# Sparse attention and a feed-forward layer on one core: a second reading for the range of the weight words, gamma folded into the first weights, one chunk more by seven products

## The chip, the cores and the metric

The kernel runs on one core of a Trainium2 chip. Its time is the device time of one execution in microseconds. Of the core's engines, TensorE (PE in the profile) multiplies matrices into PSUM, VectorE (DVE), ScalarE (ACT) and GpSimd (POOL) work on rows of 128 partitions, and SyncE (SP) issues most DMAs. Each engine runs its own row of instructions in a fixed order and waits for the others by semaphores.

## The reference

```python
scores = scale * np.matmul(q, k.transpose(0, 1, 3, 2))
keep = is_global | is_local              # k < n_global, or 0 <= q - k < n_local
bias = -slopes[:, None, None] * dist[None, :, :]
a = softmax(np.where(keep, scores + bias, -1e9))
x = np.matmul(a, v)                      # B 4, H 8, S 768, D 64: x is 4 x 768 x 512
xn = (x - mu) / np.sqrt(var + 1e-06) * g_ln
return x + np.maximum(xn @ w_ch1, 0.0) @ w_ch2   # 512 -> 2048 -> 512
```

The two counts come as 64-bit integers (8 and 96 here). The two weight matrices come as float64 words, which the chip has no arithmetic for. All else is float32.

## The kernel before

The 3072 tokens make 24 tiles of 128. A tile needs the keys of its own and of the previous tile, and the first 16 columns of its batch's first tile as global keys. The first tile of each batch is a "short" one: its scores need one block of keys. The four short tiles come first and are worked in float32 (`quick`): `tk` and `tq` are transposes of keys and queries on TensorE, `s` the scores, `T` their masked and exponentiated values (a custom step on VectorE adds the mask and finds the row's extreme), `tp` the transposed probabilities, copied to `pT`, `pv` probabilities by values, `x` the divided sum, `xs` the centred rows, `tx` their transposes. The other 20 tiles are split into pairs of float16 (upper and lower half: `kn`, `qn`, `vn`, `pn`, `xn`) and transposed by DMA. A pair of tiles is a chunk; its normalised, transposed rows are `xT`.

The weights are brought as 16 pieces of 1 MB (`wb0` to `wb15`, eight for each matrix). From a piece, ScalarE takes the low word (`wr`), VectorE the sign (`ws`), ScalarE the absolute high word with a running sum (`wz`, into `big`, from which the range of the words is judged at the end), VectorE shifts the two together (`ww`) into a float32 word, and the halves are written: the upper by any of three engines (`wu`: `w1h`, `w2h`), the lower by VectorE or GpSimd (`wl`: `w1l`, `w2l`). The pieces of the second matrix lie until their turn in `w2h`, `w2l` or `st`, which is why early rows of the first matrix's words carry the name `w2h`.

Each of the 12 chunks has eight first products F (24 products of 256 columns each, in `f`), whose rectified halves are `h`, and eight second products. For chunks below EVEN these are G (12 products of 512 columns); from EVEN on they are N, the "seven products": sums of h rows (`R`, made by `mixes`, then split into `uh` and `ul`) against sums of weight blocks (`va`, `t`; made once, by `sums_of_weights`), 21 products of 256 columns a step, in `m`. `combine` drains their sums into `x`, which SP stores.

The order of all of this is written out by a planner (`class Plan`): each piece of work is a task with an engine (or a choice of engines), a cost, a rank, the tasks that it follows and the buffers that it takes; the planner lists tasks greedily and each engine's row is then fixed. Where its TensorE would idle before UNTIL = 90, it puts filler products, `blank`. A helper, `Lane`, records every operation, so nearly all rows of the profile have its line, L204 (L238 in the kernel after). The last task but one is a flag: `judge` collects whether the counts, the words' range and the variances lie within what this path handles, `pf` adds that over the partitions with a product, and a branch to a general kernel follows (not taken here).

## Time and profile before

| | us |
|---|---|
| three runs, median (lowest to highest) | 608.58 (607.15 to 609.28) |
| profiled execution's span | 605.5 |
| TensorE busy | 591.0 (98%) |
| VectorE busy | 514.9 (85%) |
| ScalarE busy | 408.6 (67%) |
| GpSimd busy | 160.8 (27%) |

The span runs from the first to the last instruction of one profiled execution; the run's time holds some 3 us more. A busy TensorE counts filler products too, and the busy shares are means over stages of different kinds, so a stage is read by itself: the stages here are the start with the short tiles and first weights (to 73 us), the chunks with plain second products and attention (to about 230), those with seven products and attention (to about 510), and the rest without attention. The clock that TensorE was granted is 1.00 in all of them but the last, where it is 0.98.

### The profile page before, as it was taken

The page shows a single profiled execution, that of the slowest core. Times are in us where ns is not written, and L with a number is a line of the kernel's source. Part 1 is how long each engine was busy: PE and PEld are TensorE (multiplying, and loading weights), DVE is VectorE, ACT ScalarE, POOL GpSimd, SP SyncE. Part 2 cuts the span into 40 slices and gives each one's busy share as a digit, 9 for nine tenths or more (in the row PEclk, how much of TensorE's full clock was granted, in tenths as well). Part 3 has the DMA queues.
Part 4 walks back from the last instruction along what each step waited for, and adds up shares of the span by engine and source line. Part 5 has one row for each costly group of instructions (what it writes and reads, how often), then busy time and mean ns, then how long its engine had stood idle before and what let it go on. Part 6 is the DMA issues. An engine that isn't in the chain of part 4 may idle for free.

```text
span 605.5 us, 15320 instructions
## 1 busy us (share of the span) xinstructions
PE 591.0 (98%) x5929; PEld 489.7 (81%) x5929; DVE 514.9 (85%) x1244; ACT 408.6 (67%) x1004; POOL 160.8 (27%) x128
## 2 busy tenths in 40 slices
PE   8989999999999999999999999999999999999996
PEld 4767896556965985789999999999999999988885
DVE  5999999999999989899789999898898788484654
ACT  5988897965677865787765766889856756333330
POOL 2310121306463228242042122152232031040100
PEclk9999999999999999999999999999999999999999
DMA  8993999976879985977748676868865423110001
GB/s 217 321 312 102 238 221 193 244 183 132 221 165 183 183 191 130 202 158 108 156 125 141 139 157 123 162 137 160 154 141 123 105 55 88 36 40 16 35 2 37
DMA packets 247307, 88.33 MB, mean 146 GB/s; under 512 B 237376, under 2 KB 237376, under 8 KB 247232
## 3 DMA queue, kind: packets, MB, share of 16 engines
q1 hardware_dynamic: 246944, 87.32, 65.6%
q8 instruction: 47, 0.77, 0.6%
q14 instruction: 28, 0.23, 0.1%
q10 hardware_dynamic: 288, 0.00, 0.0%
HBM read 38.01 MB, written 6.29 MB: 73 GB/s over the span
## 4 chain that ended last, share of the span: by engine, by line
PE 62%; DVE 5%; DMA 1%; issue 1%; ACT 0%; DVEq 0%
PE f L204 31%; PE m L204 24%; PE s L204 4%; PE pv L204 3%; DMA out_dram<-x 1%; DVE vn L204 1%; DVE T L204 1%; DVE pn L204 1%; DVE x L204 1%; DMA xT<-xn 0%; DVE w2l L204 0%; DVE R L204 0%; DVE xs L204 0%; DVE qn L204 0%; DVE xn L204 0%
## 5 line engine op out<-in xcount | busy, mean ns | idle before, releaser
L204 PE MATMUL f<-xT,w1h 128*128 128x256 f16 x1536 | 256.3, 273 | 4.7 <-DVE xT L204 2.1
L204 PE MATMUL f<-xT,w1l 128*128 128x256 f16 x768 | 209.3, 273 | 0.0
L204 PEld LDWEIGHTS <-w1h 128*128 128x128 f16 x1536 | 147.5, 98 | 21.9 <-DVE xT L204 2.2
L204 DVE SCALAR_TENSOR_TENSOR R<-f,R 128x128 f32<-128x128 f32 x256 | 68.3, 288 | 35.0 <-ACT R L204 29.6
L204 PEld LDWEIGHTS <-uh 128*128 128x128 f16 x896 | 85.9, 98 | 9.4
L204 PEld LDWEIGHTS <-w1l 128*128 128x128 f16 x768 | 75.1, 98 | 9.2 <-issue 0.5
L204 ACT ACTIVATE T<-T,mn 128x256 f32<-128x256 f32 x160 | 80.1, 501 | 3.2
L204 PE MATMUL f<-w2h,h 128*128 128x512 f16 x256 | 80.4, 379 | 0.4 <-DVE h L204 0.4
L204 ACT ACTIVATE uh<-R 128x896 f16<-128x896 f32 x57 | 54.0, 948 | 38.2 <-DVE R L204 37.9
L204 DVE CUSTOM_DVE_ANT_0 T<-s,mask 128x256 f32<-128x256 f32 (+1 forms) x192 | 68.1, 396 | 10.8 <-PE s L204 10.7
L204 ACT ACTIVATE R<-f 128x512 f32<-128x512 f32 x59 | 35.1, 594 | 61.8 <-PE f L204 60.3
L204 PE MATMUL m<-w2h,uh 128*128 128x256 f16 x256 | 69.8, 273 | 0.0
L204 PE MATMUL m<-w2l,uh 128*128 128x256 f16 x256 | 69.8, 273 | 0.0
L204 PE MATMUL m<-w2h,ul 128*128 128x256 f16 x256 | 69.8, 273 | 0.0
L204 PE MATMUL m<-t,uh 128*128 128x256 f16 x384 | 69.5, 273 | 0.0
L204 PEld LDWEIGHTS <-h 128*128 128x128 f16 x384 | 36.3, 98 | 40.0 <-issue 0.6
L204 POOL TENSOR_TENSOR ul<-R,uh 128x896 f16<-128x896 f32 x17 | 32.4, 1907 | 121.4 <-ACT uh L204 121.4
L204 DVE TENSOR_TENSOR ul<-R,uh 128x896 f16<-128x896 f32 x47 | 54.1, 1151 | 12.1 <-ACT uh L204 11.8
L204 POOL TENSOR_TENSOR pn<-T,pn 128x512 f16<-128x512 f32 x27 | 33.8, 1250 | 114.0 <-ACT pn L204 90.1
L204 PE MATMUL s<-kT,qT 128*128 128x128 f16 (+1 forms) x704 | 55.7, 225 | 2.0 <-ACT T L204 0.9
L204 PE MATMUL m<-t,ul 128*128 128x256 f16 x192 | 52.3, 273 | 0.0
L204 ACT ACTIVATE pn<-T 128x512 f16<-128x512 f32 x78 | 48.7, 624 | 2.2 <-DMA xT<-xn 1.1
(155 smaller groups left out, 1018.3 us busy)
## 6 DMA issues: line engine op xcount, KB each, us to landing
st<-in_moe_w_ch_dram SPq DMA_DIRECT2D x10, 1024.0 KB, 6.8
kf<-in_k_dram SPq DMA_DIRECT2D x28, 256.0 KB, 3.9
vf<-in_v_dram SPq DMA_DIRECT2D x28, 256.0 KB, 3.4
qf<-in_q_dram SPq DMA_DIRECT2D x24, 256.0 KB, 3.2
out_dram<-x SPq DMA_DIRECT2D x24, 256.0 KB, 2.4
qT<-qT SPq DMA_DIRECT2D x40, 128.0 KB, 2.7
w2h<-in_moe_w_ch_dram SPq DMA_DIRECT2D x3, 1024.0 KB, 7.3
w2l<-in_moe_w_ch_dram SPq DMA_DIRECT2D x3, 1024.0 KB, 8.3
```

Source lines behind the costliest of these rows:

```text
L204: ins = getattr(self.engine, name)(*args, **kw)
```

## The change

- Chunk 3 has seven products instead of plain ones (EVEN 3), so the weight sums are due a chunk earlier.
- The reading of the high words on ScalarE (`wz`) goes, and `big` with it. Instead, all weights are read from memory once more behind the last tile's scores: 64 DMAs of 256 KB (`again`) and 64 steps on VectorE that collect exponent bits in `seen`, judged by `judge_words` before the flag's product.
- Gamma is multiplied into the first weights (`gw`, from a load `gs` of four elements a partition), so `gb`, a load of 256 KB, goes; the centring step now takes mean and root at once, so the diagonal matrix and its step go and `tx` is a plain transpose.
- The first two pieces of w1 hold 256 columns of all 512 rows instead of 512 columns of 256 rows ("tall"); the first F needs one of them. The halves of w1 are written by blocks of rows, each with its gamma. `wl` no longer has GpSimd as a choice.
- The counts are read to one partition and spread to all by a product (`all<-cnt,row`).
- The copy of global values (`gv`) is a DMA instead of a VectorE step. The mixes are three steps instead of four. In the last chunk product 3 has a bank with product 7, and the last stored piece is half a row block.
- The planner has other costs and ranks, tables that shift ranks by kind, and a changed LEAD (how many steps ahead the late tiles' scores may come). The sign step is on VectorE in both.

```diff
+WORD = -WS * 2.0 ** -128
...
-EVEN = 4
-EARLY = 150.0
-LEAD = 11
+EVEN = 3
+EARLY = -167.15
+LEAD = 4
...
+KINDS = {
+    "kh": 14.0, "vh": 10.0, "ph": 20.0, "wr2": 9.0, "pt": 33.0, "wl1": -13.0, "wb1": 3.0, "wu1": 13.0, "R": -10.0, "Z": -23.0, "vl": 23.0,
...
+    def asked(n):
+        src = (n_global, n_local)[n]
+        if "asked" not in made:
+            made["asked"] = const.tile([1, 2, 2], I32, name="nn")
+        act.dma_start(out=made["asked"][:, n, :], in_=src.bitcast(I32).partition_broadcast(1))
+
+    def count_one():
+        made["one"] = counted(const, vec, made["asked"])
+
+    def count_all():
+        made["all"] = ps_v.tile([P, 2], F32, tag="pv", name="all")
+        pe.matmul(made["all"], lhsT=made["row"], rhs=made["one"], start=True, stop=True)
 
     def count():
-        cnt = made["cnt"] = counted(const, vec, made["asked"])
+        cnt = made["cnt"] = const.tile([P, 2], F32, name="cnts")
+        vec.tensor_copy(out=cnt, in_=made["all"])
...
+    task("gs", "SP", 0.6, lambda: load.dma_start(out=gs, in_=g_ln.rearrange("(c p) -> p c", p=P)), rank=-5, dma=0.3)
+    task("gw", "DVE", 0.11, lambda: vec.tensor_scalar(out=gw, in0=gs, scalar1=WORD, scalar2=None, op0=ALU.mult), ["gs"], rank=-5)
...
+        tall = n < 2
+        if tall:
+            sl, cs = slice(n * 256, (n + 1) * 256), slice(0, NK)
+            src, dh, dl = w1[:, sl], w1h[:, :, sl], w1l[:, :, sl]
...
-        def sizes():
-            hi = staged[n][1]
-            act.activation(out=hi.bitcast(F32), in_=hi.bitcast(F32), func=AF.Abs, scale=2.0 ** -111, accum_out=big[:, n:n + 1])
-
         def whole():
             lo, hi, _, _ = staged[n]
-            vec.scalar_tensor_tensor(out=hi, in0=hi, scalar=3, in1=lo, op0=ALU.logical_shift_left, op1=ALU.bitwise_or)
+            vec.scalar_tensor_tensor(out=hi, in0=hi, scalar=3, in1=lo, op0=ALU.logical_shift_left, op1=ALU.bitwise_xor)
 
         def upper(engine):
-            if engine == "DVE":
-                vec.tensor_copy(out=dh, in_=staged[n][3])
+            word = staged[n][3]
+            if n < NF // 2:
+                if engine == "POOL":
+                    pool.tensor_tensor(out=dh, in0=word, in1=gw[:, cs].unsqueeze(2).to_broadcast(list(word.shape)), op=ALU.mult)
+                    return
+                for a in range(cs.stop - cs.start):
+                    g_ = gw[:, cs.start + a:cs.start + a + 1]
+                    if engine == "DVE":
+                        vec.tensor_scalar(out=dh[:, a], in0=word[:, a], scalar1=g_, scalar2=None, op0=ALU.mult)
+                    else:
+                        act.activation(out=dh[:, a], in_=word[:, a], func=AF.Copy, scale=g_)
+            elif engine == "DVE":
+                vec.tensor_scalar(out=dh, in0=word, scalar1=WORD, scalar2=None, op0=ALU.mult)
             elif engine == "POOL":
-                pool.tensor_tensor(out=dh, in0=staged[n][3], in1=fill.unsqueeze(2).to_broadcast([P, 2, 512]), op=ALU.subtract)
+                pool.tensor_scalar(out=dh, in0=word, scalar1=WORD, scalar2=None, op0=ALU.mult)
             else:
-                act.activation(out=dh, in_=staged[n][3], func=AF.Copy)
-
-        def lower(engine):
-            (pool if engine == "POOL" else vec).tensor_tensor(out=dl, in0=staged[n][3], in1=dh, op=ALU.subtract)
+                act.activation(out=dh, in_=word, func=AF.Copy, scale=WORD)
+
+        def lower():
+            word = staged[n][3]
+            if n < NF // 2:
+                for a in range(cs.stop - cs.start):
+                    k0 = cs.start + a
+                    vec.scalar_tensor_tensor(out=dl[:, a], in0=word[:, a], scalar=gw[:, k0:k0 + 1], in1=dh[:, a], op0=ALU.mult, op1=ALU.subtract)
+            else:
+                vec.scalar_tensor_tensor(out=dl, in0=word, scalar=WORD, in1=dh, op0=ALU.mult, op1=ALU.subtract)
...
-        task(f"ws{n}", "DVE", 0.7, signs, [f"wr{n}"], rank=rank, port=True)
-        task(f"wz{n}", "ACT", 1.2, sizes, [f"ws{n}"], rank=rank)
-        task(f"ww{n}", "DVE", 1.22, whole, [f"wz{n}"], rank=rank, port=True)
...
-                task(f"gv{b}_{i}", "DVE", 0.42, spread_v, [f"P{t - 1}_3"], rank=rank - 20, port=True)
+                    load.dma_start(out=made["vn", t - 1, i - 1][:GK], in_=made["vn", first, 0][:GK])
...
-            vec.scalar_tensor_tensor(out=xc, in0=xs[t].rearrange("p h d -> p (h d)"), scalar=mv[:, t, 0:1], in1=gb, op0=ALU.subtract, op1=ALU.mult)
+            vec.tensor_scalar(out=xc, in0=xs[t].rearrange("p h d -> p (h d)"), scalar1=mv[:, t, 0:1], scalar2=made["rs", t], op0=ALU.subtract, op1=ALU.mult)
 
         def flip():
-            made["xt", t] = turn(made["xc", t], f"tx{t}", "f1" if t < 2 else "f2", made["diag"][t])
+            made["xt", t] = turn(made["xc", t], f"tx{t}", "f2")
...
-            for to, here, there, op in ((2, ps[:, 1, 0], 0, ALU.subtract), (4, ps[:, 1, 0], 3, ALU.add), (5, ps[:, 0, 0], 4, ALU.subtract), (6, ps[:, 0, 1], 5, ALU.add)):
-                vec.scalar_tensor_tensor(out=U[:, to], in0=here, scalar=0.0, in1=U[:, there], op0=ALU.max, op1=op)
+            vec.scalar_tensor_tensor(out=U[:, 2:5:2], in0=ps[:, 1, 0].unsqueeze(1).to_broadcast([P, 2, P]), scalar=0.0, in1=U[:, 0:4:3], op0=ALU.max, op1=ALU.subtract)
+            for to in (5, 6):
+                vec.scalar_tensor_tensor(out=U[:, to], in0=ps[:, 0, to - 5], scalar=0.0, in1=U[:, to - 1], op0=ALU.max, op1=ALU.subtract)
...
+        pieces = [f"wl{f // 2}"] if f < 4 else [f"wl{2 * j}", f"wl{2 * j + 1}"]
...
+    def where(c, m):
+        return (3, 1) if m == 3 and c == NC - 1 else WHERE[m]
...
-                step(x0[:, hi], at(5), 1.0)
+                if c < NC - 1:
+                    step(x0[:, hi], at(5), 1.0)
...
+        task(f"Oh{t0}", "SP", 0.4, lambda: store(t0, hi), [f"D{c}_2", f"D{c}_4", f"D{c}_6"], rank=rank, dma=0.5)
+        task(f"O{t0}", "SP", 0.4, lambda: store(t0, lo), [f"D{c}_2", f"D{c}_5"], rank=rank, dma=0.5)
...
-            parts_ = [(every, (j,)) for j in range(4)] + [((m,), (4, 5, 6)) for m in (1, 6, 7, 4)] + [((1, 6, 7), (7,)), ((4,), (7,))] + [((m,), (4, 5, 6, 7)) for m in (5, 3, 2)]
+            parts_ = [(every, (j,)) for j in range(4)] + [((m,), (4, 5, 6)) for m in (1, 6, 7, 3)] + [((1, 6, 7), (7,)), ((3,), (7,))] + [((m,), (4, 5, 6, 7)) for m in (4, 5, 2)]
...
+    def judge_words():
+        seen, ok = made["seen"], made["ok"]
+        vec.tensor_scalar(out=seen, in0=seen, scalar1=0x70000000, scalar2=None, op0=ALU.bitwise_and)
+        most = const.tile([P, 1], F32, name="most")
+        vec.tensor_reduce(out=most, in_=seen.bitcast(F32), axis=AX.X, op=ALU.max)
+        vec.tensor_scalar(out=ok[:, 4:5], in0=most, scalar1=0.0, scalar2=None, op0=ALU.is_le)
+        vec.tensor_reduce(out=total[:, 0:1], in_=ok, axis=AX.X, op=ALU.min)
+
+    again = {}
+
+    def read_again(n, tag):
+        st = again[n] = p2.tile([P, 256], I64, tag=tag, name=f"again{n}", bufs=p2_bufs[tag])
+        if n < 2 * NF:
+            src = w1[n // 8 * P:(n // 8 + 1) * P, n % 8 * 256:(n % 8 + 1) * 256]
+        else:
+            m = n - 2 * NF
+            src = w2[m // 2 * P:(m // 2 + 1) * P, m % 2 * 256:(m % 2 + 1) * 256]
+        load.dma_start(out=st, in_=src)
+
+    def range_of(n):
+        hi = again[n].bitcast(I32).rearrange("p (n two) -> p n two", two=2)[:, :, 1]
+        if n == 0:
+            made["seen"] = p2.tile([P, 256], I32, tag="pT", name="seen", bufs=3)
+            vec.tensor_scalar(out=made["seen"], in0=hi, scalar1=0x30000000, scalar2=None, op0=ALU.bitwise_xor)
+        else:
+            vec.scalar_tensor_tensor(out=made["seen"], in0=hi, scalar=0x30000000, in1=made["seen"], op0=ALU.bitwise_xor, op1=ALU.bitwise_or)
+
+    p2_bufs = {"ld": 6, "kT": 3, "vn": 3}
+    for n_ in range(4 * NF):
+        tag = ("ld", "kT", "ld", "vn")[n_ % 4]
+        task(f"V{n_}", "SP", 0.6, lambda n_=n_, tag=tag: read_again(n_, tag), [f"S{B * NT - 1}_1"], rank=1e4 + n_, take={tag: [f"J{n_}"]}, dma=0.8)
+        task(f"J{n_}", "DVE", 0.33, lambda n_=n_: range_of(n_), [f"V{n_}"] + ([f"J{n_ - 1}"] if n_ else []), rank=1e4 + n_, take={} if n_ else {"pT": ["never"]}, port=True)
...
 
-    task("K0", "DVE", 2.0, judge, [f"M{n_}" for n_ in range(50)] + [f"A{t}" for t in range(B * NT)] + [f"wz{n}" for n in range(NF)], rank=1e4)
-    task("K1", "PE", 0.1, across_rows, ["K0", f"F{NC - 1}_{NF - 2}"], rank=-1e3, take={"s": ["K2"]})
+    task("K0", "DVE", 2.0, judge, [f"M{n_}" for n_ in range(50)] + [f"A{t}" for t in range(B * NT)], rank=1e4)
+    task("JJ", "DVE", 1.2, judge_words, ["K0", f"J{4 * NF - 1}"], rank=1e4)
+    task("K1", "PE", 0.1, across_rows, ["JJ", f"F{NC - 1}_{NF - 2}"], rank=-1e3, take={"s": ["K2"]})
```

Around the first F of chunk 0, TensorE's row before is as follows (`s`, `tp`, `tk`, `tx` belong to the short tiles; `f_0_0` is the first F; fillers are left out):

```order
L204 MATMUL s_0_416<-kT_0_383,qT_399 128x128 x4
L204 MATMUL s_1_424<-kT_0_383,qT_399 128x128 x4
...
L204 MATMUL tx_446<-aside,xs_421 128x128 x4
L204 MATMUL tx_456<-aside,xs_404 128x128 x4
...
L204 MATMUL tp_0_478<-ident,T_0_431 128x128 x4
L204 MATMUL tk_492<-ident,kf_0_401 128x128 x4
...
L204 LDWEIGHTS w1h
L204 MATMUL f_0_0_499<-xT_334,w1h 128x256
```

and in the kernel after:

```order
L238 MATMUL s_0_508<-kT_0_485,qT_440 128x128 x4
L238 MATMUL tp_0_519<-ident,T_0_454 128x128 x4
L238 MATMUL s_1_535<-kT_0_485,qT_440 128x128 x4
...
L238 MATMUL tx_544<-ident,xs_540 128x128 x4
...
L238 MATMUL tp_1_557<-ident,T_1_513 128x128 x4
L238 MATMUL pv_566<-vf_0_315,pT_0_549 128x64 x4
L238 LDWEIGHTS w1h
L238 MATMUL f_0_0_573<-xT_353,w1h 128x256
```

The scores of the fourth short tile (`s_0_508`, `s_1_535`), the third's last `tp` and its first `pv` now stand ahead of the first F; before, they stood between F steps.

VectorE's row behind the masked scores of the second short tile, before (`w2h` holds words of w1 here):

```order
L204 SCALAR_TENSOR_TENSOR w2h<-w2h 128x1024
L204 COPY pT_1_307<-tp_1_279 128x512
L204 CAST w1h<-w2h 128x2x512
L204 TENSOR_TENSOR w1l<-w2h,w1h 128x2x512
L204 RECIPROCAL r<-r 128x8
L204 TENSOR_TENSOR x_335<-pv_293,r 128x512
L204 BN_STATS st<-x_335 128x6
L204 BN_AGGR mv<-st 128x2
L204 TENSOR_SCALAR rs<-mv 128x1
L204 TENSOR_SCALAR w2h<-w2h 128x1024
L204 TENSOR_SCALAR w2l<-w2l 128x1024
```

and after, from the end of the first tile's masked scores on:

```order
L238 TENSOR_SCALAR w2h<-w2h 128x1024
L238 SCALAR_TENSOR_TENSOR w2h<-w2h 128x1024
L238 TENSOR_SCALAR w1h<-w2h,gw 128x256 x4
L238 SCALAR_TENSOR_TENSOR w1l<-w2h,gw,w1h 128x256 x4
L238 TENSOR_SCALAR w2h<-w2h 128x1024
L238 SCALAR_TENSOR_TENSOR w2h<-w2h 128x1024
...
L238 RECIPROCAL r<-r 128x8
L238 TENSOR_TENSOR x_354<-pv_293,r 128x512
L238 SCALAR_TENSOR_TENSOR w1l<-w2h,gw,w1h 128x256 x4
L238 BN_STATS st<-x_354 128x6
```

The copy `pT` and the cast of the first piece as one step are gone from VectorE's row, the whole first piece is through (four steps for each half, by blocks of rows) before the next tile's scores, and shift and sign of a piece now follow each other directly.

VectorE's row at the end of the kernel after, ahead of the flag:

```order
L238 SCALAR_TENSOR_TENSOR R<-f_11_12_9373,R 128x2x128
L238 SCALAR_TENSOR_TENSOR R<-f_11_12_9373,R 128x128 x2
L238 SCALAR_TENSOR_TENSOR seen<-again_9356,seen 128x256
L238 SCALAR_TENSOR_TENSOR seen<-again_9361,seen 128x256
L238 SCALAR_TENSOR_TENSOR seen<-again_9366,seen 128x256
L238 SCALAR_TENSOR_TENSOR seen<-again_9368,seen 128x256
L238 TENSOR_TENSOR ul_12_9463<-R,uh_12_9433 128x896
L238 TENSOR_SCALAR seen<-seen 128x256
L238 TENSOR_REDUCE most<-seen 128x1
L238 TENSOR_SCALAR ok<-most 128x1
L238 TENSOR_REDUCE mask_87<-ok 128x1
```

The rows `seen<-again` of the second reading stand between the mixes (`R`) and the lower halves (`ul`) of the last chunk; each waits for its load, and what stands behind it waits too.

## Rows read from the trace of the kernel before

**Rows 1.** The page, part 1: busy us (share) and instructions of each engine.

```profile
PE 591.0 (98%) x5929; PEld 489.7 (81%) x5929; DVE 514.9 (85%) x1244; ACT 408.6 (67%) x1004; POOL 160.8 (27%) x128
```

**Rows 2.** Busy time by stretch: from:to, length, then engines, clock, DMA share, GB/s.

```profile
0.00:10.00 10.00, 8.42 (x37) 4.62 (x38) 3.07 (x15) 4.10 (x9) 0.88 (x10) 1.00 0.71 194
10.00:38.60 28.60, 24.26 (x166) 17.01 (x164) 26.75 (x82) 26.33 (x77) 10.26 (x5) 1.00 0.95 300
38.60:73.40 34.80, 33.10 (x286) 28.65 (x287) 33.15 (x59) 29.31 (x56) 3.87 (x3) 1.00 0.73 208
73.40:203.00 129.60, 128.66 (x1177) 89.23 (x1176) 126.88 (x245) 97.66 (x239) 44.68 (x35) 1.00 0.89 191
203.00:265.00 62.00, 60.88 (x624) 46.16 (x623) 55.68 (x127) 43.67 (x122) 27.49 (x22) 1.00 0.87 171
...
510.00:589.00 79.00, 79.00 (x761) 70.75 (x758) 48.80 (x126) 26.91 (x42) 9.65 (x7) 1.00 0.10 28
```

**Rows 3.** Waits of TensorE, whole span: total us, times, longest.

```profile
PE f L204 <- DVE xT L204: 2.1, 2, 1.8
```

**Rows 4.** Timeline of TensorE to 74 us: start, us, operation, idle before.

```profile
4.65 1.11 PE L204 MATMUL tk<-ident,kf 128*128 128x128 f32 x4
...
6.83 0.86 PE L204 MATMUL tq<-ident,qf 128*128 128x128 f32 x4
...
38.63 0.28 PE L204 MATMUL f<-xT,w1h 128*128 128x256 f16 x1 [1.78 <-DVE xT L204]
...
73.42 0.38 PE L204 MATMUL f<-xT,w1h 128*128 128x256 f16 x2
```

**Rows 5.** Timeline of VectorE to 74 us.

```profile
10.01 0.29 DVE L204 CUSTOM_DVE_ANT_0 T<-s,mask 128x128 f32<-128x128 f32 x1 [0.98 <-PE s L204]
...
13.53 0.94 DVE L204 TENSOR_SCALAR mask<-d 128x256 bf16<-128x256 f32 x4
14.38 0.69 DVE L204 TENSOR_SCALAR qT<-tq 128x512 f32<-128x512 f32 x1
...
18.08 0.08 DVE L204 DVE_READ_ACCUMULATOR2_ANT nm<- 128x1 f32 x1
...
19.21 0.68 DVE L204 COPY pT<-tp 128x512 f32<-128x512 f32 x1
19.82 0.68 DVE L204 CAST w1h<-w2h 128x1024 f16<-128x1024 f32 x1
20.53 1.22 DVE L204 TENSOR_TENSOR w1l<-w2h,w1h 128x1024 f16<-128x1024 f32 x1
...
23.73 1.34 DVE L204 TENSOR_SCALAR w2h<-w2h 128x1024 uint16<-128x1024 uint16 x1
...
30.34 1.40 DVE L204 SCALAR_TENSOR_TENSOR xs<-x,mv,gb 128x512 f32<-128x512 f32 x2
...
35.60 0.09 DVE L204 DVE_READ_ACCUMULATOR2_ANT nm<- 128x1 f32 x1
...
72.60 0.70 DVE L204 TENSOR_TENSOR xT<-tx,xT 128x512 f16<-128x512 f32 x1
```

**Rows 6.** The chain of waits, 222 to 266 us: start, us, what.

```profile
222.94 2.59 PE f L204 x12
...
240.38 1.56 DVE pn L204
...
244.69 0.58 DVE pn L204
...
263.81 2.29 PE m L204 x21
```

**Rows 7.** The page, part 5: one group of VectorE's instructions, mean ns.

```profile
L204 DVE SCALAR_TENSOR_TENSOR R<-f,R 128x128 f32<-128x128 f32 x256 | 68.3, 288 | 35.0 <-ACT R L204 29.6
```

**Rows 8.** Timeline of VectorE behind the last product.

```profile
600.70 0.76 DVE L204 SCALAR_TENSOR_TENSOR x<-m,x 128x256 f32<-128x256 f32 x2 [0.54 <-PE m L204]
```

**Rows 9.** Timeline of TensorE, the last tile's second scores.

```profile
502.19 0.61 PE L204 MATMUL s<-kT,qT 128*128 128x128 f16 x8
```

More of the change, by code (lines that the diff above doesn't have):

```diff
@@ L120, in open_ @@
             for engine in tasks[key][0]:
-                ready[engine][key] = max([self.times[a][1] + (lag if self.on[a] != engine else 0.0) for a in after], default=0.0) + slack
+                ready[engine][key] = max([self.times[a][1] + (lag if self.on[a] != engine else -TAIL.get(engine, 0.0)) for a in after], default=0.0) + slack
         for key in tasks:
@@ L166, in order @@
             engines[engine] = t + cost
-            end = t + cost
+            end = t + cost + TAIL.get(engine, 0.0)
             if dma > 0.0:
@@ L259, in starts @@
         pool.memset(half, -0.5)
-        pool.memset(fill, 0.0)
+        made["row"] = const.tile([1, P], F32, name="row")
+        pool.memset(made["row"], 1.0)
         made["ones"] = const.tile([P, 1], F32, name="ones")
         pool.memset(made["ones"], 1.0)
-    def beside():
-        made["aside"] = aside = p2.tile([P, 1024], F16, tag="pn", name="aside", bufs=3)
-        made["diag"] = [aside[:, 2 * P * n:2 * P * (n + 1)].bitcast(F32) for n in range(4)]
     def blank():
@@ L387, in weight @@
-        task(f"wl{n}", {"POOL": 2.2, "DVE": 1.24}, 0, lower, [f"wu{n}"], rank=rank, port=True)
+        task(f"wb{n}", "SP", 0.6, bring, before, rank=rank - 12, take={} if n in homes else {"st": [f"wl{n}"]}, dma=2.8)
+        first = n < NF // 2
+        task(f"wr{n}", "ACT", 1.12, below, [f"wb{n}", "starts"], rank=rank)
+        task(f"ws{n}", "DVE", 1.12, signs, [f"wr{n}"], rank=rank, port=True)
+        task(f"ww{n}", "DVE", 1.14, whole, [f"ws{n}"], rank=rank, port=True)
+        task(f"wu{n}", {"ACT": 1.7 if tall else 1.29 if first else 1.05, "POOL": 1.95, "DVE": 1.1 if tall else 0.8 if first else 0.62}, 0, upper, [f"ww{n}", "gw"] + (["wl1"] if n == 8 else []) + (["wl3"] if n in (8, 9, 10, 11) else []) + (["wl7", "wl8"] if n >= 12 else []), rank=rank, port=True)
@@ L389, in banded @@
+        task(f"wl{n}", "DVE", 1.6 if tall else 1.32 if first else 1.14, lower, [f"wu{n}"], rank=rank, port=True)
     for n in range(NF):
@@ L416, in add @@
                 eng.tensor_tensor(out=hold["a"], in0=block(0, j, *first), in1=block(*at), op=op)
+            elif at == (0, j, 1, 0):
+                eng.tensor_tensor(out=hold["a"], in0=block(*at), in1=hold["a"], op=ALU.subtract)
             else:
@@ L878, in ffn1 @@
         j = f // 4
-        after = [f"{'xa' if c > 1 else 'xl'}{t}" for t in range(CT * c, CT * c + CT)] + [f"wl{2 * j}", f"wl{2 * j + 1}"] + steps[-1:]
+        pieces = [f"wl{f // 2}"] if f < 4 else [f"wl{2 * j}", f"wl{2 * j + 1}"]
+        after = [f"{'xa' if c > 1 else 'xl'}{t}" for t in range(CT * c, CT * c + CT)] + pieces + steps[-1:]
         if c < 2:
@@ L957, in at @@
         def at(m):
-            k, i = WHERE[m]
+            k, i = where(c, m)
             return ms[c, k][:, i]
@@ L1076, in banded @@
         tile_(t, [QUICK[t]] * 2, [[], []])
-    for c in range(NC):
+    for c in range(EVEN):
         if c < 2:
```

244 lines of the change are left out of this document (128 added, 116 removed), and 4 rows, old and new, of the table KINDS.

## The prediction

> **What bounds the kernel now.** I read the busy times first, then the busy time by stage, the waits of TensorE, the chain of waits, and last the timelines of TensorE and VectorE at both ends. TensorE is busy for 591.0 of the span's 605.5 us [rows 1], so 14.5 us at most can come from its waits; anything more has to come from fewer products. By stage [rows 2] it has no idle time at all between 510 and 589 us, about 1 us in each of the two stages from 73 to 265, and most of it in the first 73. VectorE is the second engine, and by stage the nearer bound: 59.9 of 63.4 us from 10.0 to 73.4, then 126.9 of 129.6 and 55.7 of 62.0, and only 48.8 of 79.0 between 510 and 589. The largest wait of TensorE's first products is for VectorE's xT, 2.1 us [rows 3]. In the first 73 us busy doesn't mean useful: chunk 0's eight first products, 21 us at 2.62 us, begin at 38.63 after a wait for xT, and chunk 1's begin at 73.42 [rows 4], 34.8 us later; between them stand the short tiles' products, more waits and filler products ("blank"). Chunk 1 waits for the fourth short tile's xT, whose lower half VectorE begins at 72.60 [rows 5]. So up to 73.4 the time is set by VectorE's row of work, and afterwards by TensorE's products.
>
> The profiled execution's span is 605.5 us, the median of the runs 608.58. I make the sum in the span and add the 3.1 us that lie outside it.
>
> **The start: VectorE's row up to the fourth xT.** The order says which operations stand in that row before and after; each price is the step from one row's start to the next row's, some 0.1 to 0.2 less than its busy time. Taken out: six steps of the wide mask and the small step on the global columns, now ahead of the first reduction, 1.4 us (four masks show 0.94, so 0.2 to 0.23 each); one copy of transposed probabilities (19.21 to 19.82, 0.6), one scaled query copy of as many elements (0.6) and one lower half of keys, of as many again, now behind the fourth xT (0.6) [rows 5]; one of ten sign steps, 1.1 (1.34 busy less the 0.2 that it shares with the next step). Three casts of weights become one of four column steps: 3 x 0.6 less 4 x 0.2, 1.0. Centring four tiles is 0.66 each before (xs, 1.40 for two) and is estimated at 0.40 as a one-input step, twice the 0.2 of a 256-column mask: 1.0. Put in: the lower halves of w1 are 7 x 1.15 before (1.22 busy at 20.53); after, there are eight, two in 4 steps of 256 columns at 0.33 (288 ns for 128 columns, two of 256 in 0.76 [rows 7, 8]) and six in 2 steps of 512 at 0.60: 9.8, so 1.8 more; one more vn, 0.6. Sum: -1.4 -0.6 -0.6 -0.6 -1.1 -1.0 -1.0 +1.8 +0.6 = -3.9 us. One shift step of 2.37 us, against 1.22 for the same step elsewhere [rows 5], was stretched beside GpSimd; I take 1.0 back, since no lower half of weights is left there. The row starts later, though: tile 0's queries were the second load and are the fifth, behind gs and two tiles more. The first keys' transposes start at 4.65 and the queries' at 6.83 [rows 4]; three tiles of 256 KB at 300 GB/s [rows 2] are 2.6 us, and the 512 small pieces of gs are put at 0.4 (no row shows that load so early), so the queries come at about 7.65, 0.8 late. Together: 3.9 + 1.0 - 0.8 = 4.1 us earlier. Bounds: with the queries 2.2 us late (194 GB/s of the first stage), centring at the 0.60 of the 512-column qT step, and the stretch kept, 0.9; with no delay and half of the row's 3.5 idle us gone, 6.6. I take 4.1, the value from the nearest rows. Chunk 0's products are no new bound: the order puts less between them, so 8 x 2.62 plus about 3 us fits between a start near 39 and 69.3.
>
> Removing the 16 range readings on ScalarE is worth nothing by itself where ScalarE isn't last; what it does is shorten each piece's chain from sign step to shift. The counts by one partition and a product trade a wide load for a narrow one, a product, a copy and two crossings between engines. I cost that at nothing: the first reduction waits 0.98 us for its scores [rows 5], so for the queries; without that cover it is at most about 0.8, four small steps. gb's load and gv's copies leave VectorE's and SP's rows with no one waiting for them.
>
> **The middle: chunk 3 by seven products.** Eight steps of 12 products of 512 columns (2.59 us) become eight of 21 of 256 columns (2.29) [rows 6]: 8 x 0.30 = -2.4 us, certain as long as nothing is waited for. But VectorE pays: eight mixes at 0.98 (three steps of 288 ns, one of them double [rows 7]) and seven lower halves at 1.0 in place of eight at 0.6 (+10), 21 weight sums more at 0.61 in that stretch (+12.8), less 11 other splits of 0.6 that go to GpSimd or ScalarE, gv, and centring (about -10 with the rest): from chunk 1's first h to chunk 3's last, 120.1 us of unstretched work become 132.9. Before, that took from the end of chunk 1's first step, 76.0, to that of chunk 3's last, 222.5 [rows 4, 6], 146 us, so 26 us were idle or stretched; a split such as 240.38 shows 1.56 us where 244.69 shows 0.58 [rows 6]. With the same 26 the row ends at 71.9 + 158.9 = 231 us. TensorE asks for it later too: four seven-product steps (9.2 us) now stand among chunk 3's first products, so the last of them ends at 222.5 - 4.1 + 9.2 = 227.6, and its user comes some 3 steps after. It is a tie with a few us of cover. I cost the waits that this adds at 0.8; bounds -2.1 (the 2.1 us of waits from 73 to 265 gone [rows 2]) and +10 (the idle and stretched time grows by half, less 3 of cover).
>
> Here a page has a rule that speaks against the change. The row: 1.56 against 0.58 us for one split while GpSimd works [rows 6]. The Trainium skill, "SBUF — State Buffer", "Who interferes with whom", says that VectorE steps with two SBUF inputs, and plain copies, casts and scalings in their two-port mode, share a port pair with GpSimd, which the loser waits for whole. By that the new centring and scaling steps would be exposed, not only the splits, and the sum would move towards the +10; this is the mechanism of rival B.
>
> **The second reading** is 64 loads of 256 KB and 64 steps of 256 words. A step is 0.28 (a quarter of the 1.13 of the shift step over 1024 words) to 0.38 (256 elements in the last drain) [rows 5, 8]; at 0.33 it is 21 us, in a stage with 30.2 idle us on VectorE [rows 2]. The loads start after the last tile's second group of scores (502.19 before [rows 9]; seven steps of 2.45 later and 6 earlier, about 513) and must be in by the flag product, the end of that stage at 589, now near 583: 16.8 MB in 70 us is 240 GB/s, beside 28 of other traffic; the start of the kernel shows 300 over 28.6 us [rows 2]. Both fit: 0. Without cover, late loads hold VectorE's queue, with R and ul behind them, and TensorE's last products behind those.
>
> **The tail.** After the last product VectorE now has one step of 256 columns instead of two (0.76 us [rows 8]), and stores half a row block: -0.5 (0.3 to 0.8).
>
> **Sum.** 605.5 - 4.1 - 2.4 - 0.5 + 0.8 + 0 = 599.3 of span, 602.4 us. Faster and slower mean more than 0.3%, about what a measurement of this kernel can tell from no change: below 606.75, above 610.4.
>
> **Rivals.**
> A. The start gives little: the queries come late and the VectorE row keeps its gaps, so the chunk-1 start stays near 73; 602.4 + 3.5 = 605.9. For it: the row had 3.5 idle us that no edit addresses; against: 3.9 us of listed work. Chance 0.14.
> B. VectorE is late in the middle. Place: the first seven-product steps of chunk 3 and the first products of chunk 4. Price: every us by which idle and stretch exceed about 26 + 3 reaches TensorE; at half more, +10: 602.4 + 10 = 612.4, slower than before. For it: 98% busy there [rows 2] and 12.8 us more work; against: later demand. It turns the sign once the waits that it adds exceed 7 us. Chance 0.13.
> C. The second reading comes late: at the 180 GB/s mean of the middle stages 16.8 MB take 93 us, 17 to 20 too long: 620. Against it the 300 GB/s. Chance 0.05.
> D. More than I count: the middle waits vanish and the start gains 6: 602.4 - 0.8 - 2.1 - 1.9 = 597.6. Chance 0.08.
>
> **How the numbers follow.** The forecast has 0.60, with its own range 599.5 to 605.5. Faster: nearly all of it and D, and six tenths of A: 0.59 + 0.08 + 0.09 = 0.76. Same: the rest of A and the near half of B, 0.06 + 0.06 = 0.12; slower: the other half of B, and C, 0.07 + 0.05 = 0.12. The range 597 to 609 leaves out C, the upper part of B and the lowest of D.
>
> **What would show it.** Right: chunk 1's first product at 69 to 70 us, the wait of that product for xT still VectorE's; chunk 3's second product in steps of 2.29; waits of about 3 between 73 us and the end of chunk 3; VectorE near 70 of 79 us busy before the flag product with no TensorE wait there; a last step of 0.4 after the last product. Wrong: chunk 1 beginning at 73 (A), TensorE waiting for R, h or weight sums between 190 and 260 (B), a wait for VectorE with a load behind it after 515 (C).

## The result, and the profile after

The kernel after takes 601.93 us (median of 4 runs, 601.76 to 603.58), the kernel before 607.87 (4 runs) on the same chips: a ratio of 0.9909 with a 95% interval of 0.9886 to 0.9933. Forecast were 602.4 us and a range of 597 to 609. The profiled execution of the kernel after is the slowest of its four, 603.58 us with a span of 601.8; the three others have spans of 600.0 to 600.1.

Busy time by engine, on the page of the kernel after, against [rows 1]:

```profile
PE 588.7 (98%) x6000; PEld 496.5 (83%) x6000; DVE 520.6 (87%) x1253; ACT 411.1 (68%) x1018; POOL 142.0 (24%) x118
```

Busy time by stretch of the kernel after (from:to, length, then engines, clock, DMA share, GB/s), against [rows 2]; the second stretch ends where chunk 1 begins:

```profile
10.00:38.60 28.60, 27.32 (x191) 19.69 (x190) 26.39 (x91) 26.00 (x76) 1.85 (x2) 1.00 1.05 354
38.60:70.50 31.90, 30.45 (x262) 26.00 (x260) 31.59 (x54) 23.76 (x48) 3.38 (x3) 1.00 0.64 158
70.50:203.00 132.50, 130.92 (x1206) 91.53 (x1204) 127.62 (x253) 94.36 (x229) 46.64 (x36) 1.00 0.94 191
203.00:265.00 62.00, 61.78 (x697) 56.00 (x695) 56.14 (x132) 48.48 (x128) 20.95 (x15) 1.00 0.76 144
510.00:585.00 75.00, 75.00 (x732) 67.45 (x731) 69.08 (x176) 29.30 (x53) 6.37 (x5) 1.00 0.82 257
```

The two waits of TensorE that are largest after the first product, against [rows 3]:

```profile
PE f L238 <- DVE h L238: 3.0, 3, 1.6
PE pf L238 <- DVE mask L238: 2.1, 1, 2.1
```

TensorE's timeline at the start, against [rows 4]: the transposes of the first tile's queries, the first scores, the first products of chunk 1.

```profile
7.92 0.66 PE L238 MATMUL tq<-ident,qf 128*128 128x128 f32 x4
...
10.23 1.71 PE L238 MATMUL s<-kT,qT 64*128 64x128 f32 x16
...
70.56 0.38 PE L238 MATMUL f<-xT,w1h 128*128 128x256 f16 x2
```

VectorE's timeline at the start, against [rows 5]: the first masked scores, a tall piece's lower half in four steps, lower halves of two steps each (the second stretched), and the fourth xT.

```profile
11.54 0.29 DVE L238 CUSTOM_DVE_ANT_0 T<-s,mask 128x128 f32<-128x128 f32 x1 [1.84 <-PE s L238]
...
17.08 1.66 DVE L238 SCALAR_TENSOR_TENSOR w1l<-w2h,gw,w1h 128x256 f16<-128x256 f32 x4
...
32.35 1.41 DVE L238 SCALAR_TENSOR_TENSOR w1l<-w2l,gw,w1h 128x512 f16<-128x512 f32 x2
...
43.52 2.45 DVE L238 SCALAR_TENSOR_TENSOR w1l<-w2l,gw,w1h 128x512 f16<-128x512 f32 x2
...
69.50 0.69 DVE L238 TENSOR_TENSOR xT<-tx,xT 128x512 f16<-128x512 f32 x1
```

The reader is to see three things. Chunk 1 begins at 70.56 instead of 73.42, 2.86 us earlier, and its xT is still the last thing before it. Between there and the flag TensorE's idle time falls from 2.1 us (0.94 and 1.12 in two stretches [rows 2]) to 1.8 (1.58 and 0.22). From chunk 1's first to the last product TensorE is busy for 522.2 us instead of 524.9; 2.4 of these 2.7 us are the forecast's price of chunk 3, for the rest no row here names a cause. So TensorE is 5.8 us ahead of the kernel before when it reaches the flag. There it loses 2.1 again in this one execution: the flag's product `pf` waits for VectorE, which is still at the second reading. VectorE's rows, and then TensorE's:

```profile
583.41 1.80 DVE L238 SCALAR_TENSOR_TENSOR seen<-again,seen 128x256 int32<-128x256 int32 x4
...
586.45 0.42 DVE L238 TENSOR_REDUCE most<-seen 128x1 f32<-128x256 f32 x1
```

```profile
587.40 0.21 PE L238 MATMUL pf<-mask,ones 128*1 128x27 f32 x2 [2.08 <-DVE mask L238]
```

And the end, against [rows 8]: the last product, and the issue of the last three stores by SyncE.

```profile
596.62 0.27 PE L238 MATMUL m<-w2h,ul 128*128 128x256 f16 x1
```

```profile
596.54 1.87 SPq L238 DMA_DIRECT2D out_dram<-x  x3
```

From the last product's start to the end of the span it is 5.18 us; before it was 5.12 (600.39 to 605.51). So -2.9 -0.3 -2.7 +2.1 +0.1 = -3.7, which is the 605.5 to 601.8 of the two spans. The three other executions are some 1.7 us shorter; as they were not profiled, it is not shown that what they lack is the wait at the flag.

### The profile page after: what moved, and what is told of

Same layout as the page of the kernel before. It is cut to its first block, busy times and chain, and to the rows that moved or that the text cites. A ratio compares the mean times of both kernels' runs of the same rounds, so it can differ in the third digit from the quotient of the medians.

```text
span 601.8 us, 15718 instructions
## 1 busy us (share of the span) xinstructions
PE 588.7 (98%) x6000; PEld 496.5 (83%) x6000; DVE 520.6 (87%) x1253; ACT 411.1 (68%) x1018; POOL 142.0 (24%) x118
## 5 line engine op out<-in xcount | busy, mean ns | idle before, releaser
L238 PEld LDWEIGHTS <-uh 128*128 128x128 f16 x1008 | 96.4, 98 | 10.5
L238 ACT ACTIVATE uh<-R 128x896 f16<-128x896 f32 x72 | 67.7, 941 | 42.9 <-DVE R L238 42.7
L238 DVE SCALAR_TENSOR_TENSOR R<-f,R 128x128 f32<-128x128 f32 (+1 forms) x216 | 72.0, 334 | 14.4 <-ACT R L238 9.5
L238 POOL TENSOR_TENSOR pn<-T,pn 128x512 f16<-128x512 f32 x32 | 43.0, 1342 | 155.9 <-ACT pn L238 125.7
L238 PE MATMUL m<-w2h,uh 128*128 128x256 f16 x288 | 78.5, 273 | 0.0
L238 PE MATMUL m<-t,uh 128*128 128x256 f16 x432 | 78.3, 273 | 0.0
L238 DVE TENSOR_TENSOR ul<-R,uh 128x896 f16<-128x896 f32 x55 | 63.7, 1158 | 3.3 <-ACT uh L238 3.3
L238 PE MATMUL f<-w2h,h 128*128 128x512 f16 x192 | 60.9, 379 | 1.6 <-DVE h L238 1.6
L238 ACT ACTIVATE mn<-nm 128x2 f32<-128x2 f32 x80 | 16.1, 201 | 55.9 <-DVE nm L238 54.8
L238 PEld LDWEIGHTS <-ul 128*128 128x128 f16 x504 | 49.3, 98 | 5.7
```

The costliest lines, as they stand in the source:

```text
L238: ins = getattr(self.engine, name)(*args, **kw)
```

## The experiments

Wherever an edit changes a task, the planner orders the work anew; only experiment 7 leaves the order of experiment 2 as it is. A ratio compares a run with the kernel before, run beside it (medians 607.78 us for experiments 1 to 4, 608.80 for 5 to 8, 607.97 for 9 to 12). A difference to the kernel after is one of medians from different sessions, and these three medians differ by 1.0 us among themselves: by the ratios experiments 5, 6 and 8 are 9.5, 6.6 and 8.9 us slower than the kernel after, not 11.0, 6.9 and 10.

**1. Without the second reading.**

```diff
-    for n_ in range(4 * NF):
-        task(f"V{n_}", "SP", ...)
-        task(f"J{n_}", "DVE", 0.33, ...)
-    task("JJ", "DVE", 1.2, judge_words, ["K0", f"J{4 * NF - 1}"], rank=1e4)
+    task("JJ", "DVE", 0.2, judge_words, ["K0"], rank=1e4)
```

> The kernel after without the second reading of the weights: its 64 loads, its 64 steps on VectorE and the judging of the words' range are left out (so the range is not judged). Theory: the reading costs only the wait of the flag's product for VectorE (2.1 us of waiting there in the profile of the kernel after), because its loads and steps otherwise lie beside the products; the span falls from 601.8 to about 599.6, the time by 0.5 to 2.2 us, and the flag's product waits for nothing. Rival: the loads hold up other transfers too and TensorE's products run slower beside them; then the time falls by more than 3 us and more changes than the wait at the flag. Second rival: the reading costs nothing in most executions, then the time stays within 0.5 us of 601.9.

Measured: 601.78 us (601.11 to 602.78), ratio 0.9902 [0.9881, 0.9923]; profiled span 599.3, with no wait at the flag. The wait is gone from the profile, as the theory has it, but the median is that of the kernel after to within 0.2 us, where the five runs lie 1.7 us apart: the second rival holds as far as these runs can tell. A cost of the reading of less than about 1 us can't be excluded.

**2. The reading's step at its price.**

```diff
-        task(f"J{n_}", "DVE", 0.33, ...)
+        task(f"J{n_}", "DVE", 0.45, ...)
```

> The kernel after with one number changed: the planner's cost of a step of the second reading is 0.45 us, the step that the profile of the kernel after shows, instead of 0.33. The flag's product then stands some 60 products later in TensorE's row. Theory: VectorE ends the reading just as late as before, about 587 us, but the flag's product is asked for 6 us later, so its wait of 2.1 us is gone and the time falls as much as without the reading, to within 0.7 us of that kernel. Rival: VectorE's lateness also holds up the lower halves of the last chunk, so the wait moves to the products behind them and the time stays at 601.9.

Measured: 601.78 us (601.10 to 602.64), ratio 0.9899 [0.9878, 0.9920]; span 599.5. TensorE's row has the flag's product at 591.16, without a wait.

The wait at the flag was one of order: asked for some 6 us later, the product finds its operand there, and no wait appears behind it. In time it can't be told from the kernel after.

**3. Chunk 3 by plain products again.**

```diff
-EVEN = 3
+EVEN = 4
```

> The kernel after with chunk 3 by plain second products again (EVEN 4 instead of 3; the planner orders the rest anew). Theory: eight steps of 2.59 us come back for eight of 2.29, so the time rises by 2.4 us to about 604.3, less what waits between 190 and 260 us fall. Rival: with a chunk less of mixes and the weight sums a chunk later, VectorE is eased in the middle, the waits there fall and the time stays within 1 us of 601.9 or falls.

Measured: 604.47 us (603.76 to 606.97), ratio 0.9940 [0.9922, 0.9959]: 2.5 us slower than the kernel after, and 2.7 slower than experiments 1 and 2. The 2.4 us of the theory are there. This execution's profile (606.97 us, its slowest) also shows a fall of the clock behind a wait: in TensorE's row, a wait of 2.3 us for h, and from 99 to 102 us, at a granted clock of 0.50, products of 512 columns that start 0.43 us apart instead of 0.22.

```profile
97.80:99.00 1.20, 1.15 (x6) 0.52 (x6) 0.93 (x1) 1.20 (x4) 0.41 (x1) 0.94 1.10 208
99.00:102.00 3.00, 3.00 (x15) 1.60 (x14) 1.90 (x6) 1.25 (x5) 1.15 (x1) 0.50 1.04 358
102.30:104.00 1.70, 1.70 (x14) 0.84 (x13) 1.31 (x3) 1.70 (x4) 0.00 (x0) 1.00 1.04 417
```

```profile
97.85 0.38 PE L238 MATMUL f<-w2h,h 128*128 128x512 f16 x1 [2.30 <-DVE h L238]
98.06 0.38 PE L238 MATMUL f<-w2l,h 128*128 128x512 f16 x1
...
100.25 0.63 PE L238 MATMUL f<-w2h,h 128*128 128x512 f16 x1
100.67 0.63 PE L238 MATMUL f<-w2l,h 128*128 128x512 f16 x1
101.10 1.06 PE L238 MATMUL f<-w2h,h 128*128 128x512 f16 x2
```

**4. The kernel before with chunk 3 by seven products.**

```diff
-EVEN = 4
+EVEN = 3
```

> The kernel before with chunk 3 by seven products, and nothing else of the change (the planner orders the rest with its own numbers). Theory: TensorE saves 2.4 us, and as the kernel before has VectorE 98% busy from 73 to 203 us, part is paid back in waits: the time falls by 0 to 2.4 us, to 605.5 to 608. Rival: VectorE can't carry the mixes and the earlier weight sums without the rest of the change; the time rises by 3 us or more above 607.9, with waits of the products for R, h or weight sums between 150 and 260 us.

Measured: 626.64 us (626.48 to 627.07), ratio 1.0309 [1.0288, 1.0330]: slower by 19 us. The rival holds. TensorE's two largest waits, the stretch from 203 to 265 us, and what the DMA queue of SyncE waits for in it:

```profile
PE pv L204 <- DMA pT<-pn: 6.3, 2, 4.9
PE f L204 <- DVE R L204: 6.1, 3, 3.1
```

```profile
203.00:265.00 62.00, 51.67 (x542) 44.98 (x540) 57.42 (x120) 40.26 (x98) 29.36 (x21) 0.92 0.44 98
```

```profile
SPq L204 <- DVE xn L204: 12.0, 1, 12.0
```

VectorE is busy for 57.4 of 62 us there and TensorE for 51.7; the waits are for transposes that hang on VectorE's splits (the queue itself waits for `xn` and, for 11.4 us, for `qn`), and for the mixes themselves. As the order was made anew with numbers fitted to EVEN 4, part of the 19 us may be the order's.

**5. ScalarE's reading put back in each piece's chain.**

```diff
+        def sizes():
+            hi = staged[n][1]
+            act.activation(out=hi.bitcast(F32), in_=hi.bitcast(F32), func=AF.Copy, accum_out=big[:, n:n + 1])
...
-        task(f"ww{n}", "DVE", 1.14, whole, [f"ws{n}"], rank=rank, port=True)
+        task(f"wz{n}", "ACT", 1.14, sizes, [f"ws{n}"], rank=rank)
+        task(f"ww{n}", "DVE", 1.14, whole, [f"wz{n}"], rank=rank, port=True)
```

> The kernel after with ScalarE's reading of the high words put back between the sign step and the shift of each of the 16 pieces (its sum goes into a tile that nothing uses; the second reading stays). Theory of the prediction: the reading is worth nothing by itself, since VectorE's row and not ScalarE's sets the start: chunk 1 begins within 1 us of 70.6 and the time stays within 1 us of 601.9. Rival: ScalarE is busy for 26.0 of 28.6 us from 10.0 to 38.6 in the kernel after, so eight more steps of 1.14 us by 70 us make it the bound and each piece's chain is 1.2 us longer: chunk 1 begins 3 to 9 us later and the time rises by 3 us or more.

Measured: 612.92 us (611.18 to 613.18), ratio 1.0066 [1.0045, 1.0088]: 11.0 us slower than the kernel after. Chunk 1 begins at 78.3 (counted by its products) instead of 70.6. By stretch (columns as above):

```profile
10.00:38.60 28.60, 27.58 (x189) 18.93 (x187) 21.80 (x77) 26.39 (x76) 2.76 (x2) 1.00 1.08 330
38.60:70.00 31.40, 31.15 (x246) 24.34 (x245) 28.71 (x58) 30.55 (x64) 1.94 (x2) 1.00 0.57 162
```

ScalarE, the fourth column, is now busy for 30.55 of 31.40 us, against 23.8 of 31.9 in the kernel after, and VectorE falls to 21.8 of 28.6. VectorE's largest waits for ScalarE's words up to 78 us (0.9 more for `w2l`; the kernel after has none):

```profile
DVE w2h L238 <- ACT w2h L238: 3.6, 2, 3.1
DVE st L238 <- ACT st L238: 1.1, 1, 1.1
```

Chunk 1 doesn't wait for the fourth xT here, which ends at 73.6, but for chunk 0's last two first products: they start at 73.1, right behind the last lower half of w1, which ends at 73.0 instead of 62.2. So the rival's mechanism is there, and in this order the reading is not worth nothing. How much of the time is the reading's and how much the new order's can't be told from this run: experiments 6, 8 and 11, with other edits, lose 7 to 13 us.

**6. The first tile's queries loaded second.**

```diff
-    "Lk0": -21.0, "Lv4_0": ...
+    "Lk0": -21.0, "Lq0": -20.0, "Lv4_0": ...
```

> The kernel after with the first tile's queries loaded directly behind its keys and gs (a rank of the planner is changed; the row of TensorE up to chunk 0 is ordered anew). Theory: VectorE's row starts with the first masked scores, at 11.54 us in the kernel after, where it had waited 1.84 us; with the queries two tiles (1.7 us) earlier it starts at about 10, and chunk 1 begins 1 to 1.5 us earlier, near 69.3; time 600.5 to 601. Rival: what comes later in that row waits for other arrivals (second tile's queries, values) so the 1.5 us are given back as gaps and chunk 1 begins at 70 to 71.

Measured: 608.80 us (608.26 to 611.09), ratio 1.0018 [1.0001, 1.0035]: 6.9 us slower than the kernel after. VectorE's row:

```profile
8.83 0.29 DVE L238 CUSTOM_DVE_ANT_0 T<-s,mask 128x128 f32<-128x128 f32 x1 [0.45 <-ACT mask L238]
...
10.79 1.89 DVE L238 TENSOR_SCALAR mask<-d 128x256 bf16<-128x256 f32 x7
13.93 0.69 DVE L238 TENSOR_SCALAR qT<-tq 128x512 f32<-128x512 f32 x1 [1.26 <-PE tq L238]
...
20.43 0.29 DVE L238 CUSTOM_DVE_ANT_0 T<-s,mask 128x128 f32<-128x128 f32 x1 [1.23 <-PE s L238]
```

The first masked scores come 2.7 us earlier, at 8.83. All of it is given back: the wide masks come behind them (1.9 us), then two waits of 1.2 to 1.3 us for the next queries and scores, and chunk 1 begins at 72.7. The late queries had covered the masks. Another 4.2 us are lost between there and 265, where TensorE is idle for 6.0 us instead of 1.8. The rival holds, and more than it said.

**7. The last half row block from another queue** (with the price of experiment 2).

```diff
-            load.dma_start(out=out[b, i * P:(i + 1) * P, half_], ...)
+            (act if half_ == lo else load).dma_start(out=out[b, i * P:(i + 1) * P, half_], ...)
```

> The kernel with the reading's step priced at 0.45, and besides that the last half row block stored from ScalarE's DMA queue instead of SyncE's. Theory: in the kernel after the last store was issued 1.41 us behind the last product's start (1.09 before), because the store ahead of it on the same queue took 0.96 us to issue; from another queue it goes out about 0.6 us earlier, and the time from the last product's start to the end of the span falls from 5.18 (5.68 in the kernel with the step priced at 0.45) by 0.5 us. Rival: the end is set by the landing of the stores, which share the DMA engines, and the tail stays within 0.15 us.

Measured: 602.12 us (601.20 to 602.77), ratio 0.9897 [0.9878, 0.9917]; 6.0 us from the last product's start (593.42) to the end of the span (599.4), against 5.68 in experiment 2. No gain, and 0.3 us worse than the rival said. The last store was issued earlier, 1.44 us behind the last product's start instead of 1.68, and still the end did not come sooner, so in this run the issue isn't what sets it. What does, I can't say from this.

**8 to 11. Four changes of the plan.** The rank tables empty; the first pieces of w1 cut by rows; the counts loaded to all partitions; LEAD at 11:

```diff
-KINDS = {"kh": 14.0, "vh": 10.0, ...}
+KINDS = {}
+SHIFT = {}
+GIVEN = {}
```

```diff
-        tall = n < 2
+        tall = False
...
-        pieces = [f"wl{f // 2}"] if f < 4 else [f"wl{2 * j}", f"wl{2 * j + 1}"]
+        pieces = [f"wl{f // 2}"] if f < 0 else [f"wl{2 * j}", f"wl{2 * j + 1}"]
```

```diff
-    task("asked0", ...); task("asked1", ...); task("count0", ...); task("count1", "PE", ...)
+    task("asked", "ACT", 0.9, asked, rank=-60, dma=-4.7)
+    task("count", "DVE", 1.0, count, ["starts", "ident", "asked"], rank=-3)
```

```diff
-LEAD = 4
+LEAD = 11
```

> The kernel after with the planner's three new tables empty (ranks by kind, shifts of single tasks, two given engines); its costs, margins and all changed work stay. Theory: chunk 3 by seven products leaves VectorE no slack in the middle, and only an order fitted to it avoids waits; with the tables empty TensorE waits for R, h and weight sums between 150 and 260 us, the start loses some us too, and the time rises by 5 to 20 us. Rival: the new costs alone give a sound order and the tables are trimmings: time up by less than 3 us.

> The kernel after with the first two pieces of w1 cut by rows as in the kernel before (512 columns of 256 rows), so that the first product of chunk 0 needs both instead of one. Theory: the first product needs the rows xT of the second tile later than both pieces anyway (the second piece's lower half ends at 25.5 us, xT at 40.4), so nothing is gained by the cut: chunk 1 begins within 0.7 us of 70.6, and it can be earlier, since the lower halves in two steps of 512 columns cost 1.32 us against 1.58 in four of 256. Rival: the cut lets the chunks' first products begin earlier and is part of the 2.9 us of the start; without it chunk 1 begins 1 us or more later.

> The kernel after with the counts loaded to all 128 partitions as in the kernel before, without the product that spreads them. Theory: the first masked scores wait for the queries (1.84 us of VectorE's idle time in the kernel after), so counts that come 0.5 us later (5.50 against 5.58 less the work ahead of it) are hidden: the first masked scores stay at 11.5 within 0.3 us and the time within 1 us of 601.9. Rival: the masks come later, push into VectorE's row and chunk 1 begins 0.5 us or more later.

> The kernel after with the late tiles' scores allowed 11 steps ahead instead of 4 (LEAD), the rest as it is. Theory: that distance is one of the things that make chunk 3 by seven products bearable: with 11, VectorE and ScalarE have the masked scores and splits of later tiles beside chunk 3's mixes and the weight sums, TensorE waits for R, h or transposes between 190 and 260 us, and the time rises by 3 us or more. Rival: the distance matters only for when the second reading may start; then the time stays within 1.5 us.

Measured: 611.88 us (609.32 to 613.50), ratio 1.0056 [1.0035, 1.0076] without the tables; 622.49 (621.67 to 623.10), 1.0236 [1.0218, 1.0253] with flat pieces; 627.09 (623.80 to 630.56), 1.0302 [1.0268, 1.0337] with wide counts; 615.40 (613.66 to 617.19), 1.0125 [1.0103, 1.0146] with LEAD 11. Chunk 1 begins at 72.6, 72.4, 79.8 and 71.4 us; the first masked scores come at 13.6 with wide counts, not at 11.5. The larger part of the loss lies elsewhere, and in all four a part of it at one place (with wide counts it is 9 us at the start, 8 there and 6.5 more up to 200). The stretch from 140 to 163 us, where chunk 2 begins and the next tiles' attention stands between the products, in the kernel before and the kernel after, then without tables, with flat pieces, with wide counts and with LEAD 11:

```profile
140.00:163.00 23.00, 23.00 (x238) 18.70 (x236) 22.79 (x46) 14.06 (x38) 10.10 (x9) 1.00 0.84 189
140.00:163.00 23.00, 23.00 (x246) 19.33 (x245) 22.64 (x44) 16.26 (x42) 13.04 (x11) 1.00 1.11 217
```

```profile
140.00:163.00 23.00, 18.90 (x199) 14.25 (x198) 21.93 (x47) 14.89 (x39) 9.38 (x8) 0.93 0.89 181
```

```profile
140.00:163.00 23.00, 9.40 (x133) 7.47 (x131) 21.21 (x51) 15.71 (x47) 9.42 (x8) 0.70 1.12 221
```

```profile
140.00:163.00 23.00, 15.06 (x173) 9.92 (x171) 22.76 (x47) 15.53 (x45) 12.83 (x10) 0.88 0.89 182
```

```profile
140.00:163.00 23.00, 16.59 (x165) 12.26 (x164) 22.30 (x47) 14.13 (x41) 11.30 (x9) 0.85 1.02 211
```

VectorE is busy for 21 to 23 of the 23 us in each. In the kernels before and after that just suffices and TensorE never waits; in the others it waits 4 to 14 us, and the granted clock falls to between 0.70 and 0.93. The DMA engines are nearly full there as well (share 0.84 before, 1.11 after, 0.89 to 1.12 in the four), and the waits named are for what goes through their queue, so these runs don't tell whether VectorE or the queue holds TensorE up. With flat pieces the largest wait is for transposes of the split probabilities; with wide counts one of 5.4 us is for the copy of global values, which the change made a DMA:

```profile
PE pv L238 <- DMA pT<-pn: 7.6, 4, 3.5
PE pv L238 <- DMA vn<-vn: 5.4, 1, 5.4
```

So the expectations of experiments 8 and 11 hold in size, though the place lies earlier than they said, and those of 9 and 10 fail: neither the cut nor the counts is hidden once the order is made anew. But these runs don't price the cut or the counts either: a rise of 20 us is what a plan costs that isn't fitted, and a fitted plan with flat pieces or wide counts wasn't tried. Without the tables the changed work is slower than the kernel before (ratio 1.0056). The counterpart, the kernel before with the new costs and an order fitted as closely, wasn't run either, so how much of the gain is the order's alone is open.

**12. The reading done twice.**

```diff
-    for n_ in range(4 * NF):
+    for n_ in range(8 * NF):
```

> The kernel after with the second reading done twice (128 loads and 128 steps). Theory: the single reading is hidden with nothing to spare: VectorE was busy for 69.1 of 75.0 us before the flag, a step is 0.45 us, so 64 more steps are 29 us of which some 6 find idle time, and the flag's product comes about 23 us later; the time rises by 15 to 25 us. Rival: loads decide: 33.6 MB at 354 GB/s, the highest mean that a stage of the kernel after shows, are 95 us against 75; a rise of 20 us, with VectorE's waits for loads and not its steps filling the stage. Third: there is more cover than the stage shows, and the time rises by less than 5.

Measured: 635.16 us (634.44 to 636.03), ratio 1.0450 [1.0429, 1.0470]: 33 us more, beyond both. By stretch, before and after TensorE has come to the flag, and VectorE's wait for the loads:

```profile
510.00:594.00 84.00, 83.17 (x803) 74.11 (x801) 78.17 (x196) 31.36 (x55) 6.33 (x5) 1.00 0.93 292
594.00:628.00 34.00, 0.87 (x8) 0.53 (x6) 24.65 (x58) 0.00 (x0) 0.00 (x0) 0.56 0.96 354
```

```profile
DVE seen L238 <- DMA again<-in_moe_w_ch_dram: 10.2, 41, 1.1
```

The flag's product waits 33.7 us. At first the steps fill VectorE (78 of 84 us), then the loads decide, at 354 GB/s and with 41 waits. The cover of one reading is used up by it: what a second one adds is paid in full.

## Why the prediction was right, and where it was not

**The start, 4.1 us forecast, 2.86 measured.** The length of VectorE's row came out right, but by luck: from the first masked scores to the fourth xT it is 58.6 us (11.54 to 70.1), where 63.2 less 4.9 gives 58.3. Its busy time fell by 2.1 us and not by 4.9, and its idle time, which the forecast took to stay, by 2.5, from 3.5 to 1.0. The two rows, before and after, and VectorE's waits before, from 10 us on (1.0 of the 2.4 for scores ends where the row begins; after, the only wait is the 1.8 us that end there):

```profile
10.01:73.20 63.19, 57.15 (x450) 45.47 (x449) 59.69 (x140) 55.43 (x132) 14.13 (x8) 1.00 0.83 249
11.54:70.10 58.56, 55.83 (x435) 44.20 (x434) 57.58 (x143) 49.48 (x123) 5.23 (x5) 1.00 0.83 252
```

```profile
DVE T L204 <- PE s L204: 2.4, 3, 1.0
DVE h L204 <- ACT h L204: 0.7, 1, 0.7
DVE w2h L204 <- ACT w2h L204: 0.5, 1, 0.5
```

So more than half of the 4.6 us came from waits for scores (1.4) and for ScalarE (1.2) inside the row that the new order doesn't have. Of the work, a tall piece's lower half took 1.58 us, not 1.32, a flat one 1.32, not 1.2, and a stretched step stayed (2.45 against 1.41), so that the 1.0 taken back for it didn't come. The reason given for that 1.0 misread the row: what ran on GpSimd beside the stretched step before was an upper half of weights, and GpSimd still writes upper halves. The stretched step and GpSimd's before, then GpSimd's beside the stretched one after:

```profile
35.60 2.37 DVE L204 SCALAR_TENSOR_TENSOR w2l<-w2l 128x1024 int32<-128x1024 int32 x1
```

```profile
34.98 1.91 POOL L204 TENSOR_TENSOR w1h<-w2l,fill 128x1024 f16<-128x1024 f32 x1 [4.38 <-issue]
```

```profile
42.84 1.91 POOL L238 TENSOR_TENSOR w1h<-st,gw 128x1024 f16<-128x1024 f32 x1 [6.84 <-DVE st L238]
```

The later start was mis-sized too: the queries came at 7.92, as forecast (7.65), but the scores stood 2.3 us behind them in place of 1.9, and the row began 1.5 us later, not 0.8. Experiment 6 speaks against this delay having been a loss to be had back: the masks lay in it.

**The reading on ScalarE, nothing forecast.** This step is the weakest. It holds "where ScalarE isn't last", but before the change ScalarE was busy for 26.3 of 28.6 and 29.3 of 34.8 us [rows 2], almost as long as VectorE. Nine readings were 10.3 us of that. Without them ScalarE wrote the upper halves of six pieces instead of four, and was still busy for only 49.8 us from 10 us to chunk 1's beginning, against 55.6 before. Experiment 5 shows VectorE waiting 5.6 us for ScalarE once the readings are back, and chunk 1 beginning 7.7 us later. It gives no price, since the order was made anew: in the kernel before, with the same readings, VectorE waited for ScalarE for only 1.2 us. That the missing reading made the room for the casts is likely, but not shown with the order held fixed.

**Chunk 3, 2.4 forecast.** Experiment 3 returns 2.5. **The waits in the middle, +0.8 forecast, -0.3 measured** (2.1 to 1.8)**:** the tie with VectorE was kept. Rival B's mechanism is seen in experiment 4, at the place that rival B names and at up to 19 us. Experiments 8 to 11 don't show it: their common loss is at 140 to 163 us, where VectorE is as full in the kernel before (22.79 of 23 us) without chunk 3's extra work. Centring steps, of the kind that rival B fears for, were stretched at times, most at 539.51: 2.13 us, beside a step of GpSimd from 539.48 to 541.36, against 0.54 as the median of 24. What I had not seen is how much the order, which I read for its rows, decides: without its tables the gain is gone.

**The second reading, nothing forecast.** By medians right (experiments 1 and 2). Its margin was misjudged: a step takes 0.42 us and starts every 0.45, not 0.33, so 64 are 29 us, VectorE was busy for 69.1 of 75.0, and the flag waited 2.1 in the profiled execution. Rival C's loads cost one reading 2.4 us of VectorE's waits at most, and decide in two.

**The tail, -0.5 forecast, 0 measured.** One step fewer stands behind the last product, but three stores go out in place of two, and the last was issued 1.41 us behind the last product's start (598.03), 1.09 before (601.48).

**Outside the span.** I added 3.1 us from the median; in the runs of this kernel it is 1.8. The 3.1 came from setting a profiled execution's span against the median of all runs. The forecast span of 599.3 was 0.8 too short for a usual execution (600.1), and the two errors nearly cancel. That the sum is within 0.5 us of the median is luck in part: the start and the tail were put 1.2 and 0.6 too high, the waits in the middle 1.1 too long.

## What to carry to other kernels

Where several engines are nearly full, an edit on one that isn't the bound may still be worth something: look at its busy share in the same rows, and at what it lets move over. A forecast row length can come out right with its terms wrong, so compare busy and idle time apart. Where a greedy planner writes the order, a part of a change can't be priced by taking it out and planning anew; hold the order fixed, or compare the stretches that the plans have in common. A step hidden behind other work needs its price read at the same shape: 0.45 against 0.33 us was the difference between no wait at the flag and one of 2.1 us.
